# Winograd convolution with batch normalisation on one core: first weight loads in halves, no filling matmuls, last stores on three queues

## The chip, the cores and the metric

The kernel runs on one NeuronCore of a Trainium2 chip. A core has five engines with instruction streams of their own: TensorE (PE) multiplies matrices, VectorE (DVE) and ScalarE (ACT) work elementwise and can read the accumulators in PSUM, GpSimd (POOL) works elementwise on SBUF, and SyncE (SP) issues DMA transfers. ACT and POOL can issue transfers too. Each engine works through its own list in order and waits on semaphores for the others.

The metric is the device time of one execution in microseconds (us). Three executions of the kernel before took 197.62, 198.06 and 198.07 us; the median, 198.06 us, is the time to compare with. The profiled execution has a span of 196.3 us from its first to its last instruction.

## What is computed

A one-dimensional convolution with three taps over 1024 channels, a batch normalisation, and SiLU:

```python
# x: (2, 2048, 1024), w: (3, 1024, 1024), mean/var/g/b: (1024,), all bf16
xp = jnp.pad(x, ((0, 0), (1, 1), (0, 0)))
y = sum(jnp.einsum('bsc,cd->bsd', xp[:, k:k + S, :], w[k]) for k in range(3))
inv_std = 1.0 / jnp.sqrt(var + 1e-5)
y = (y - mean) * (g * inv_std) + b
return silu(y)                       # (2, 2048, 1024) bf16
```

## The kernel before

The kernel is a Winograd convolution: six output rows (`R = 6`) are made from eight transformed inputs (`NJ = 8`), so that eight products do the work of eighteen. It has three stages.

**Stage 1, the transform of x.** Each batch of x comes in 17 windows of up to 128 rows (256 KB each, the window named 16 only 66 KB). The order is windows 1 to 16, then 0. A window is one or two "jobs": a full window is two jobs of four matmuls against the transform matrix `rm`, each followed by one copy from PSUM to `T_sb` on ACT or DVE. That is 33 jobs for each batch and 66 in all. The first 48 run before the first product; the last 18 are strewn among the products of the first unit.

```python
W0_AT = (3, 4, 5)
W0_USE = 10
W1_AT = (5, 8, 11)                   # stands unused here
AMONG = 18                           # jobs left for the first unit
XBUFS = 12                           # window buffers
SPARE = 160
WARM = {0: 17, 4: 3, 6: 3, 8: 5, 10: 5}
PARAMS = 24
...
for i, wi in enumerate(order):
    load_x(0, wi)                    # one window, issued by SP
    if i in W0_AT:
        load_w(0, (0, 2, 1)[W0_AT.index(i)])   # 256 output channels of one tap: 512 KB
...
def warm(bank, n):                   # matmuls on zeros whose result nobody reads
    for _ in range(n):
        nc.tensor.matmul(
            ps[:, bank, 512 - SPARE:512], lhsT=nothing[:, 0:P], rhs=nothing, start=True, stop=True
        )

def ahead(jobs, job_n):
    for job in jobs:
        if job_n in WARM:
            warm(job_n % 4 * 2, WARM[job_n])
        t_job(job, job_n % 4 * 2)
        if job_n == PARAMS:
            params()                 # PE turns the 32 rows of var, g, mean, b; ACT copies them
        if job_n == PARAMS + 2:
            scales()                 # scale and beta of the normalisation, on POOL
        if job_n == W0_USE:
            prepare_first(0)         # Winograd weights of the first 128 channels, on POOL and ACT
        job_n += 1
```

The four rows `var`, `g`, `mean`, `b` (8 partitions of 256 bytes each) are loaded by four transfers on the POOL queue.

**Stage 2, the products.** There are 16 units, one for each block of 128 output channels (`dc`, eight of them) and batch (`bi`, two). A unit has 8 products of 8 matmuls with 342 columns, the Winograd output combinations on ACT and DVE, and a SiLU on ACT that writes its rows to `yts[bi]`. POOL makes the weights of the next channel blocks meanwhile. A finished unit is turned by a transposing DMA on SP (`turn`) and stored by SP (`store`), except the last two.

**Stage 3, the end.** The last unit is cut into parts `a` (229 columns) and `b` (113 columns). The rows of the last but one unit (`prev`) and of `a` and `b` are turned on PE (`flip`), copied from PSUM to SBUF, and stored (`ship`). A store is a list of transfers with runs of 256 bytes (128 channels):

```python
a, b = Unit(dc, bi, 4, 0, SPLIT), Unit(dc, bi, 0, SPLIT, NB)     # both write yts[bi]
sp, ac, po = nc.sync, nc.scalar, nc.gpsimd                       # ac and po are not used below
...
oa, ob, op = (olast.tile([P, R, NK, P], BF16, name=f"o{q}") for q in range(3))
...
before.store()                                       # unit 13: six transfers on SP
...
prev.flip(op, full, (0, R - 1), 1, act)
for k in range(NK):
    prev.ship(op, full[k], k * P, rows, (sp, sp, sp))     # unit 14: five transfers
...
a.flip(oa, ablocks, (0, R - 1), 5, dve)
a.ship(oa, ablocks[0], 0, rows, (sp, sp))            # one transfer, 192 KB
a.ship(oa, ablocks[1], P, rows, (sp, sp))            # two: 144 KB, then 7.5 KB
b.flip(ob, bblocks, rows, 1, dve)
b.ship(ob, bblocks[0], SPLIT, rows, (sp, sp))        # two: 168 KB, then 0.5 KB
```

Of the kernel before, what the change touches and what calls it, by code (L numbers as in the profile page):

```python
# [11 lines left out]
BF16 = mybir.dt.bfloat16  # L12
# [3 lines left out]
P = 128  # L16
R = 6
NJ = 8
W0_AT = (3, 4, 5)
W0_USE = 10  # L20
W1_AT = (5, 8, 11)
AMONG = 18
XBUFS = 12
SPLIT = 229
SPARE = 160
WARM = {0: 17, 4: 3, 6: 3, 8: 5, 10: 5}
PARAMS = 24
WT = 21

@with_exitstack  # L30
def kernel(
# [10 lines left out]
    nc = tc.nc  # L42
    B, S, C = x.shape
    D = w.shape[2]
    CT, DC = C // P, D // P
    NB = -(-S // R)
# [24 lines left out]
    T_sb = tpool.tile([P, CT, NJ, NT], BF16, name="T_sb")  # L71

    rows = consts.tile([4 * DC, P], BF16, name="rows")
    dummy = consts.tile([P, 2], FP32, name="dummy")
    nc.vector.memset(dummy, 0.0)
    nothing = consts.tile([P, SPARE], BF16, name="nothing")
    nc.vector.memset(nothing, 0.0)
    nc.scalar.activation(dummy[:, 1:2], dummy[:, 0:1], ACT.Silu)

    def transform_matrix():  # L80
# [43 lines left out]
    def load_x(bi, wi):  # L124
        if wi == 0:
            xw = xfirst
            cut = (P - 1) // 16 * 16
            nc.sync.dma_start(out=xw[1:1 + cut, :], in_=x[bi, 0:cut, :])
            nc.sync.dma_start(out=xw[1 + cut:P, :], in_=x[bi, cut:P - 1, :])
        else:  # L130
            xw = xpool.tile([P, C], BF16, name="xw")
            lo = R * WT * wi - 1
            hi = min(lo + P, S)
            nc.sync.dma_start(out=xw[0:hi - lo, :], in_=x[bi, lo:hi, :])  # L134
        clock["dma"] += 730.0
        xwin[bi, wi] = xw, clock["dma"]
# [6 lines left out]
    def load_w(pair, k, half=None):  # L143

        if (pair, "tile") not in raw:
            raw[pair, "tile"] = wpools[pair % 2].tile([P, 3, CT, 2, P], BF16, name=f"wch{pair % 2}")
        wch = raw[pair, "tile"]
        h0, h1 = (0, 2) if half is None else (half, half + 1)
        cols = slice((2 * pair + h0) * P, (2 * pair + h1) * P)
        nc.sync.dma_start(  # L150
            out=wch[:, k, :, h0:h1].rearrange("p c h d -> p c (h d)"), in_=w_all[:, k, :, cols]
        )
        clock["dma"] += 1200.0 * (h1 - h0)
        for h in range(2):
            raw[2 * pair + h] = wch[:, :, :, h]
# [74 lines left out]
    ident = consts.tile([P, P], BF16, name="ident")  # L230
    make_identity(nc, ident)

    for q, ap in enumerate((var, g, mean, b)):
        nc.gpsimd.dma_start(out=rows[q * DC:(q + 1) * DC, :], in_=ap.rearrange("(dc p) -> dc p", p=P))

    def params():

        v = ps[:, 7].bitcast(BF16)[:, 0:4 * DC]
# [15 lines left out]
    def t_jobs(bi):  # L254

        for wi in order:
            n = LAST if wi == NW - 1 else WT
            rows = min(P, S - (R * WT * wi - 1))
            n0 = bi * NB + wi * WT
            nb = 1 if CT * NJ * n <= 512 else 2  # L260
            nct = CT if nb == 1 else CT // 2
            for c0 in range(0, CT, nct):
                yield xwin[bi, wi], rows, n, n0, c0, nct, nb
# [30 lines left out]
    class Unit:  # L294
# [6 lines left out]

        def __init__(self, dc, bi, b0, lo=0, hi=NB):
            self.dc, self.bi, self.b0, self.lo, self.hi = dc, bi, b0, lo, hi
            self.bank = [ps[:, b0 + q, lo:hi] for q in range(4)]
            self.low, self.mid, self.high = (ps[:, b0 + q:b0 + q + 2, lo:hi] for q in range(3))
            self.yT = yts[bi]

        def product(self, q, j, add, between):  # L310
            dc = self.dc
# [164 lines left out]
    for i, wi in enumerate(order):  # L476
        load_x(0, wi)
        if i in W0_AT:
            load_w(0, (0, 2, 1)[W0_AT.index(i)])

    def warm(bank, n):

        for _ in range(n):
            nc.tensor.matmul(
                ps[:, bank, 512 - SPARE:512], lhsT=nothing[:, 0:P], rhs=nothing, start=True, stop=True
            )

    def ahead(jobs, job_n):
        for job in jobs:
            if job_n in WARM:  # L490
                warm(job_n % 4 * 2, WARM[job_n])
            t_job(job, job_n % 4 * 2)
            if job_n == PARAMS:
                params()
            if job_n == PARAMS + 2:
                scales()
            if job_n == W0_USE:
                prepare_first(0)
            job_n += 1
# [2 lines left out]
    ahead(jobs0, 0)  # L502
    for i, wi in enumerate(order):
        load_x(1, wi)
    jobs1 = list(t_jobs(1))
    ahead(jobs1[:-AMONG], len(jobs0))

# [29 lines left out]
            before.store()  # L537
        before, prev = prev, unit
    dc, bi = seq[-1]
    a, b = Unit(dc, bi, 4, 0, SPLIT), Unit(dc, bi, 0, SPLIT, NB)  # L540
    sp, ac, po = nc.sync, nc.scalar, nc.gpsimd
    rows = tuple(range(R))
    full = [(k * P, P, k) for k in range(NK)]
    ablocks, bblocks = [(0, P, 0), (SPLIT - P, P, 1)], [(SPLIT, NB - SPLIT, 0)]
    oa, ob, op = (olast.tile([P, R, NK, P], BF16, name=f"o{q}") for q in range(3))
    dve, act = nc.vector.tensor_copy, nc.scalar.copy
    a.scratch()
    b.scratch(a)
# [11 lines left out]
    b.plus(0, 3, between, 4.0)  # L560
    prev.flip(op, full, (0, R - 1), 1, act)
    for k in range(NK):
        prev.ship(op, full[k], k * P, rows, (sp, sp, sp))
    a.plus(2, 5, between)
    b.minus_one(between)
    a.minus_half(between)
# [9 lines left out]
    b.last(between)  # L576
    a.flip(oa, ablocks, (0, R - 1), 5, dve)
    a.ship(oa, ablocks[0], 0, rows, (sp, sp))
    a.ship(oa, ablocks[1], P, rows, (sp, sp))
    b.flip(ob, bblocks, rows, 1, dve)  # L580
    b.ship(ob, bblocks[0], SPLIT, rows, (sp, sp))

_INS = ['x', 'w', 'mean', 'var', 'g', 'b']
_OUTS = [((2, 2048, 1024), 'bfloat16')]
# [24 lines left out]
```

## Time and profile before

| what | value |
|---|---|
| median time of three executions | 198.06 us |
| span of the profiled execution | 196.3 us |
| PE busy | 181.5 us (92% of the span) |
| DVE, ACT, POOL busy | 155.2, 112.3, 138.3 us |
| read from HBM, written to HBM | 14.82 MB, 8.39 MB |
| copies of the transform jobs on ACT | 37 of 744 ns each |
| copies of the transform jobs on DVE | 29 of 844 ns each |
| matmuls of the transform jobs | 256, 25.5 us busy |

"Busy" is the time in which an engine works on an instruction. It says little alone: an engine that is idle costs time only where it is what the others wait for. The chain that ended last, followed back from the last instruction, says what the time was spent on in sequence. The time line gives the start and the length of each instruction or run of equal instructions; transfers appear there with the time that the issuing engine took to issue them ("SPq", or "POOL ... DMA_DIRECT2D"), not with the time of the data. The data are seen in the table of windows, whose last two columns are the mean share of the 16 DMA engines and the GB/s moved. In that table "PEclk" is the granted TensorE clock, 1.00 being full.

### The profile page before, as it was taken

How to read it: one execution, taken by the hardware profiler on the slowest of the kernel's cores; microseconds unless marked ns; L12 is line 12 of the kernel's file. 1: busy time of each engine (PE TensorE's matmuls, PEld its weight loads, DVE VectorE, ACT ScalarE, POOL GpSimd, SP SyncE). 2: the span in 40 equal slices, each digit the busy share in tenths (PEclk: the TensorE clock that was granted, in tenths of full speed). 3: DMA queues.
4: the chain of work that ended last, by engine and by line, in shares of the span. 5: the costliest groups of instructions: out<-in, count | busy, mean ns of one | idle time of the engine just before them, and what ended most of it. 6: DMA issues, size and time to landing. Idle time of an engine off the chain costs nothing.

```text
span 196.3 us, 3770 instructions
## 1 busy us (share of the span) xinstructions
PE 181.5 (92%) x1430; PEld 129.6 (66%) x1430; DVE 155.2 (79%) x222; ACT 112.3 (57%) x187; POOL 138.3 (70%) x80
## 2 busy tenths in 40 slices
PE   7549899999999999999999999999999999999860
PEld 6439677766666666666666666666666666679750
DVE  6636896589978799998798899889689978664760
ACT  3539897783628383547546554556273635468460
POOL 8149999962799669999999999999997750000000
PEclk9966999999999999999999999999999999999995
DMA  5999896029060929398849467959659291929644
GB/s 180 323 347 341 291 355 227 0 80 244 3 120 3 185 44 206 85 293 196 158 91 207 91 140 206 274 114 186 118 111 181 50 203 38 208 45 190 135 96 94
DMA packets 83702, 31.71 MB, mean 162 GB/s; under 512 B 67236, under 2 KB 79524, under 8 KB 83684
## 3 DMA queue, kind: packets, MB, share of 16 engines
q1 hardware_dynamic: 83556, 31.47, 67.4%
q8 instruction: 11, 0.18, 0.4%
q14 instruction: 7, 0.06, 0.1%
q0 software_dynamic: 128, 0.01, 0.0%
HBM read 14.82 MB, written 8.39 MB: 118 GB/s over the span
## 4 chain that ended last, share of the span: by engine, by line
PE 84%; SPq 4%; DMA 3%; ACT 3%; DVE 2%; issue 1%; ACTq 0%; DVEq 0%
PE ps L318 74%; PE ps L272 9%; DMA xw<-in_x_dram 3%; SPq L134 3%; ACT yT_145 L341 1%; PE ps L426 1%; DVE T_sb L285 1%; ACT T_sb L283 1%; SPq L150 1%; DVE ps L336 1%; ACT o_2156 L427 0%; DVE o_2155 L427 0%; ACTq L604 0%; ACT pc L329 0%; PE ps L239 0%
## 5 line engine op out<-in xcount | busy, mean ns | idle before, releaser
L329 ACT COPY pc<-ps 128x342 f32<-128x342 f32 (+2 forms) x34 | 14.5, 427 | 32.1 <-PE ps L318 29.5
L283 ACT CAST T_sb<-ps 128x672 bf16<-128x672 f32 (+1 forms) x37 | 26.1, 744 | 11.4 <-PE ps L272 11.2
L285 DVE CAST T_sb<-ps 128x672 bf16<-128x672 f32 (+1 forms) x29 | 23.5, 844 | 10.8 <-PE ps L272 10.3
L272 PE MATMUL ps<-rm,xw 128*128 128x168 bf16 (+1 forms) x256 | 25.5, 246 | 5.6 <-DMA xw<-in_x_dram 4.8
L272 PEld LDWEIGHTS <-xw 128*128 128x128 bf16 (+1 forms) x256 | 20.8, 103 | 10.7 <-DMA xw<-in_x_dram 6.3
L341 ACT ACTIVATE yT_145<-ps,beta,scale 128x342 bf16<-128x342 f32 (+5 forms) x27 | 18.4, 689 | 7.6 <-PE ps L318 7.6
L336 DVE SCALAR_TENSOR_TENSOR ps<-ps,pc 128x342 f32<-128x342 f32 (+2 forms) x34 | 16.9, 498 | 7.3 <-PE ps L318 5.7
L341 ACT ACTIVATE yT_144<-ps,beta,scale 128x342 bf16<-128x342 f32 (+1 forms) x24 | 17.4, 732 | 5.9 <-PE ps L318 5.9
L336 DVE SCALAR_TENSOR_TENSOR sd<-pc,ps 128x342 f32<-128x342 f32 (+2 forms) x17 | 8.3, 488 | 14.7 <-ACT sd L329 14.7
L329 ACT COPY sd<-ps 128x342 f32<-128x342 f32 (+2 forms) x17 | 7.3, 429 | 9.9 <-PE ps L318 9.8
L331 ACT ACTIVATE pc<-ps 128x342 f32<-128x342 f32 (+2 forms) x17 | 7.5, 441 | 9.4 <-PE ps L318 5.8
L318 PE MATMUL ps<-T_sb,wch_1539 128*128 128x342 bf16 (+2 forms) x80 | 10.8, 279 | 0.5 <-DVE ps L336 0.4
L318 PE MATMUL ps<-T_sb,wch_156 128*128 128x342 bf16 x64 | 10.6, 308 | 0.0
L318 PE MATMUL ps<-T_sb,wch_1121 128*128 128x342 bf16 x64 | 10.6, 307 | 0.0
L318 PE MATMUL ps<-T_sb,wch_710 128*128 128x342 bf16 x64 | 10.6, 307 | 0.0
L318 PEld LDWEIGHTS <-wch_1539 128*128 128x128 bf16 x80 | 7.1, 97 | 3.2 <-issue 0.9
L318 PEld LDWEIGHTS <-wch_156 128*128 128x128 bf16 x64 | 6.2, 97 | 3.1
L318 PEld LDWEIGHTS <-wch_710 128*128 128x128 bf16 x64 | 6.2, 97 | 3.1
L318 PEld LDWEIGHTS <-wch_1121 128*128 128x128 bf16 x64 | 6.2, 97 | 3.1
L198 POOL TENSOR_TENSOR u_700<-e_698,w1x_696 128x1024 bf16<-128x1024 f32 x2 | 4.2, 2132 | 5.7 <-DVE e_698 L180 5.7
L178 POOL TENSOR_TENSOR e_274<-wch_156 128x1024 f32<-128x1024 bf16 x1 | 2.1, 2113 | 6.5 <-DMA wch_156<-in_w_dram 6.5
L318 PE MATMUL ps<-T_sb,u_276 128*128 128x342 bf16 x32 | 6.1, 308 | 0.3 <-DVE T_sb L285 0.3
(262 smaller groups left out, 494.6 us busy)
## 6 DMA issues: line engine op xcount, KB each, us to landing
xw<-in_x_dram SPq DMA_DIRECT2D x30, 256.0 KB
out_dram<-o SPq DMA_DIRECT2D x28, 192.0 KB
out_dram<-o SPq DMA_DIRECT2D x14, 120.0 KB
wch_156<-in_w_dram SPq DMA_DIRECT2D x3, 512.0 KB
wch_710<-in_w_dram SPq DMA_DIRECT2D x3, 512.0 KB
wch_1121<-in_w_dram SPq DMA_DIRECT2D x3, 512.0 KB
wch_1539<-in_w_dram SPq DMA_DIRECT2D x3, 512.0 KB
xfirst<-in_x_dram SPq DMA_DIRECT2D x2, 224.0 KB
```

Of the source, the lines that this page charges most:

```text
L134: nc.sync.dma_start(out=xw[0:hi - lo, :], in_=x[bi, lo:hi, :])
L150: nc.sync.dma_start(out=wch[:, k, :, h0:h1].rearrange("p c h d -> p c (h d)"), in_=w_all[:, k, :, cols])
L178: eng.tensor_tensor(e, w0, w2, op=ALU.add)
L198: nc.gpsimd.tensor_tensor(u[:, i], sums[dc, q], o, op=op)
L272: nc.tensor.matmul(v[:, c * nb // nct, c % (nct // nb)], lhsT=xw[0:rows, (c0 + c) * P:(c0 + c + 1) * P], rhs=rm[0:rows, :, 0:n], start=Tru ...
L283: nc.scalar.copy(dst, src)
L285: nc.vector.tensor_copy(dst, src)
L318: nc.tensor.matmul(self.bank[q], lhsT=lhsT, rhs=T_sb[:, ct, j, nsl], start=not add and ct == 0, stop=ct == CT - 1, skip_group_check=add,)
L329: nc.scalar.copy(dst, self.bank[q])
L331: nc.scalar.mul(dst, self.bank[q], by)
L336: nc.vector.scalar_tensor_tensor(out=out, in0=in0, scalar=scalar, in1=in1, op0=ALU.mult, op1=op1)
L341: nc.scalar.activation(self.yT[:, rows, self.lo:self.hi], src, ACT.Silu, bias=beta[:, dc:dc + 1], scale=scale[:, dc:dc + 1])
```

## The change

The change rearranges the start and the end of the kernel; the middle stays as it is.

- At the start, the weights of the first 256 channels are loaded in halves of 128 channels: three transfers of 256 KB for the channels used first (after windows 4, 6 and 8 of the count from 0, in place of three of 512 KB after 3, 4 and 5), and the other three among the windows of the second batch. This lets more windows of x come before the weights.
- The matmuls on zeros are left out.
- The four parameter rows are issued first thing on the ACT queue and turned right after the first job (in place of after job 24), and their arithmetic on POOL comes after job 4.
- The first weights are prepared after job 18 in place of job 10.
- At the end, the five stores of the last but one unit are issued by POOL, one of the last unit's small stores by POOL and one by ACT. This is to have several issuers in place of one.
- The last unit writes its rows to a buffer of its own, and the three output tiles lie in the weight tile that is free by then.

```diff
-W0_AT = (3, 4, 5)
-W0_USE = 10
+W0_AT = (4, 6, 8)
+W0_USE = 18
 W1_AT = (5, 8, 11)
-SPARE = 160
-WARM = {0: 17, 4: 3, 6: 3, 8: 5, 10: 5}
-PARAMS = 24
 [...]
     rows = consts.tile([4 * DC, P], BF16, name="rows")
+    for q, ap in enumerate((var, g, mean, b)):
+        nc.scalar.dma_start(out=rows[q * DC:(q + 1) * DC, :], in_=ap.rearrange("(dc p) -> dc p", p=P))
     dummy = consts.tile([P, 2], FP32, name="dummy")
     nc.vector.memset(dummy, 0.0)
-    nothing = consts.tile([P, SPARE], BF16, name="nothing")
-    nc.vector.memset(nothing, 0.0)
 [...]
-    for q, ap in enumerate((var, g, mean, b)):
-        nc.gpsimd.dma_start(out=rows[q * DC:(q + 1) * DC, :], in_=ap.rearrange("(dc p) -> dc p", p=P))
 [...]
-        def __init__(self, dc, bi, b0, lo=0, hi=NB):
+        def __init__(self, dc, bi, b0, lo=0, hi=NB, yT=None):
-            self.yT = yts[bi]
+            self.yT = yts[bi] if yT is None else yT
 [...]
         if i in W0_AT:
-            load_w(0, (0, 2, 1)[W0_AT.index(i)])
+            load_w(0, (0, 2, 1)[W0_AT.index(i)], 0)
-    def warm(bank, n):
-        [...]
     def ahead(jobs, job_n):
         for job in jobs:
-            if job_n in WARM:
-                warm(job_n % 4 * 2, WARM[job_n])
             t_job(job, job_n % 4 * 2)
-            if job_n == PARAMS:
+            if job_n == 0:
                 params()
-            if job_n == PARAMS + 2:
+            if job_n == 4:
                 scales()
 [...]
         load_x(1, wi)
+        if i in W1_AT:
+            load_w(0, W1_AT.index(i), 1)
 [...]
-    a, b = Unit(dc, bi, 4, 0, SPLIT), Unit(dc, bi, 0, SPLIT, NB)
+    yT = olast.tile([P, R, NBP], BF16, name="yTlast")
+    a, b = Unit(dc, bi, 4, 0, SPLIT, yT), Unit(dc, bi, 0, SPLIT, NB, yT)
 [...]
-    oa, ob, op = (olast.tile([P, R, NK, P], BF16, name=f"o{q}") for q in range(3))
+    free = (DC // 2) % 2
+    turned = wpools[free].tile([P, 3, CT, 2, P], BF16, name=f"wch{free}").rearrange("p k c h d -> p (k c h) d")
+    op, oa, ob = (
+        turned[:, R * lo:R * hi].rearrange("p (i k) d -> p i k d", i=R)
+        for lo, hi in ((0, NK), (NK, NK + 2), (NK + 2, NK + 3))
+    )
 [...]
-        prev.ship(op, full[k], k * P, rows, (sp, sp, sp))
+        prev.ship(op, full[k], k * P, rows, (po, po, po))
 [...]
-    a.ship(oa, ablocks[1], P, rows, (sp, sp))
+    a.ship(oa, ablocks[1], P, rows, (sp, po))
 [...]
-    b.ship(ob, bblocks[0], SPLIT, rows, (sp, sp))
+    b.ship(ob, bblocks[0], SPLIT, rows, (sp, ac))
```

More of the change, by code (lines that the diff above doesn't have):

```diff
@@ L478 @@
         if i in W0_AT:
-            load_w(0, (0, 2, 1)[W0_AT.index(i)])
-    def warm(bank, n):
[L483 to L486, printed above, removed]
+            load_w(0, (0, 2, 1)[W0_AT.index(i)], 0)
     def ahead(jobs, job_n):
         for job in jobs:
-            if job_n in WARM:
-                warm(job_n % 4 * 2, WARM[job_n])
             t_job(job, job_n % 4 * 2)
-            if job_n == PARAMS:
+            if job_n == 0:
                 params()
-            if job_n == PARAMS + 2:
+            if job_n == 4:
                 scales()
```

## The prediction

> **What bounds the kernel now.** I read the page first, for the busy shares and for the chain that ended last. The second line is the chain by line: L318 is the products, L272 the transform of x.
>
> ```profile
> PE 181.5 (92%) x1430; PEld 129.6 (66%) x1430; DVE 155.2 (79%) x222; ACT 112.3 (57%) x187; POOL 138.3 (70%) x80
> PE ps L318 74%; PE ps L272 9%; DMA xw<-in_x_dram 3%; SPq L134 3%; ACT yT_145 L341 1%; PE ps L426 1%; DVE T_sb L285 1%; ACT T_sb L283 1%; SPq L150 1%; DVE ps L336 1%; ACT o_2156 L427 0%; DVE o_2155 L427 0%; ACTq L604 0%; ACT pc L329 0%; PE p
> ```
>
> The products are three quarters of the span. Then I read the same chain in order of time (start us, length us, what), to see where it leaves PE.
>
> ```profile
> 8.15 6.79 DMA xw<-in_x_dram
> 14.99 4.24 PE ps L272 x36
> ...
> 30.25 0.30 PE ps L318
> ...
> 43.66 134.97 PE ps L318 x936
> ```
>
> From 43.66 to 178.63 PE does nothing but 936 matmuls of products, 144 ns each. The change touches no instruction there, so that block moves as a whole. What can change is the start, up to the first product at 30.25, and the end, after 178.63.
>
> At the start a window of x is waited for until 14.99. The time line of PE (start, length, what, idle before) shows how the windows come: windows 5, 6 and 7 at 10.07, 12.54 and 14.99. One transform takes 0.76 us at the first and 1.30 us at the others.
>
> ```profile
> 7.57 0.51 PE L484 MATMUL ps<-nothing 128*128 128x160 bf16 x5
> 10.07 0.76 PE L272 MATMUL ps<-rm,xw 128*128 128x168 bf16 x8 [1.99 <-DMA xw<-in_x_dram]
> 12.54 1.30 PE L272 MATMUL ps<-rm,xw 128*128 128x168 bf16 x8 [1.37 <-DMA xw<-in_x_dram]
> 14.99 1.30 PE L272 MATMUL ps<-rm,xw 128*128 128x168 bf16 x8 [1.15 <-DMA xw<-in_x_dram]
> ```
>
> After 14.99 no wait for x is left: the copies bound it (ACT 744 ns, DVE 844 ns, side by side 1/(1/744 + 1/844) = 396 ns a job). Six windows, 12 jobs, are done by then. The other 36 take 36 x 0.396 = 14.2 us, and ACT's two preparing instructions (1.06 and 1.04 us, shared by two engines) 1.05 us: 14.99 + 15.3 = 30.3. The first product starts at 30.25, so the account closes.
>
> How fast data move I took from the table of windows; the last two columns are the DMA share and GB/s. At 43 to 48 only weights with runs of 512 bytes are moved, at 14 to 17 mostly x with runs of 2 KB, at 182.5 to 184 stores with runs of 256 bytes.
>
> ```profile
> 43.00:48.00 5.00, 4.99 (x35) 3.21 (x34) 4.25 (x7) 2.89 (x5) 0.00 (x0) 1.00 1.16 306
> 14.00:17.00 3.00, 2.01 (x15) 2.01 (x16) 1.41 (x2) 2.79 (x5) 2.64 (x3) 0.50 1.06 389
> 182.50:184.00 1.50, 1.49 (x23) 1.47 (x22) 0.74 (x3) 0.21 (x1) 0.00 (x0) 1.00 1.00 214
> ```
>
> The DMA engines are full in all three, and shorter runs carry less. At the end the time line of SP shows the issuing (start, length).
>
> ```profile
> 187.62 0.63 SPq L448 DMA_DIRECT2D out_dram<-o_2156  x1
> 189.82 2.52 SPq L442 DMA_DIRECT2D out_dram<-o_2154  x3
> 192.45 0.62 SPq L442 DMA_DIRECT2D out_dram<-o_2155  x1
> 193.12 0.65 SPq L448 DMA_DIRECT2D out_dram<-o_2155  x1
> ```
>
> SP had finished the last but one unit's stores at 188.25 and waited for `oa`. The copy of `ob` ends at 191.20 (190.64 + 0.56), but its store is issued at 192.45, behind three others.
>
> **What the Trainium skill says.**
>
> - "DMA: Bandwidth & Descriptors", section "Why small descriptors are slow (HBM only)": each packet costs a fixed extra, some 27% at 256 bytes. The trace agrees in direction: 214 GB/s at 256 bytes, 306 at 512, 389 at 2 KB. This bears on the halves: 256 KB then come in 256-byte runs.
> - The same page, section "Issuing engines are not separate DMA queues": several issuers save only the time of issuing. Here that time is about 0.65 us each, and only those after 191.20 count.
> - The same page, section "SWDGE vs HWDGE vs iDMA": descriptors of POOL's transfers are computed by its own cores in software. The four small ones of this kernel take 0.52 to 0.76 us each on POOL, for 8 partitions of 256 bytes; no line shows one with 768 pieces, as a store of 128 rows by 6 has.
> - "TensorE: Matmul & The Clock Gate", section "Part 1: The HAM clock gate (the "warmup" mystery)": half the clock until about 3.4 us of sustained work. The trace agrees: 0.76 against 1.30 us for the same eight matmuls, at a granted clock of 1.00 and 0.50.
>
> **The change part by part.**
>
> *Weights in halves.* By the rates above a window takes 0.262 MB / 389 = 0.67 us of transfer, a 512 KB load 0.524 / 306 = 1.71 us, and a half, if loads of 256-byte runs go like stores (an estimate), 0.262 / 214 = 1.22 us. Window 7 came after 7 windows and 3 loads, 9.86 us of transfer, at 14.99; so 5.1 us are start and delay. The check: window 5 at 5 x 0.674 + 1.71 + 5.1 = 10.2 (seen 10.07), window 6 at 12.6 (seen 12.54). With the change, window 5 comes at 8.5, 6 at 10.4, 7 at 11.0, 8 at 12.9, 9 at 13.6, and 10, behind three halves, at 10 x 0.674 + 3.67 + 5.1 = 15.5. Window 25, the last that the 48 jobs need, comes behind four halves at about 26.3, in time. So at 15.5 not 12 but 18 jobs are done. 30 jobs are left: 30 x 0.396 + 1.05 = 12.9, and the first product starts at 28.4 in place of 30.25: **-1.8 us at best**.
>
> *Parameters first.* PE, in order, stands after job 0 until four transfers issued by ACT have landed. Issuing takes about 0.45 us each, as SP's first do, from 0.72 to 2.5. The same rows took 5.6 to 6.9 us from issue to landing on POOL's queue, but amid full traffic; at the very start I take 3 us. PE then waits until about 5.5 with window 1 half done. ACT's table load (1.28 us) moves behind the issues and still ends before the first copy at 4.55. This is hidden as long as PE catches up by 15.5.
>
> *No matmuls on zeros.* 33 matmuls go, all in waits; that gives nothing back. What they bought was the clock: without them the first windows run at 1.30 us. From 5.5, five windows are ready or near, and PE works at the slow clock for one or two of its windows, until 9 to 12, then faster than the data come. Costs 0 to 1.1 us (the 0.55 us that each of two windows loses), if PE is slow again when window 10 comes.
>
> *Preparation.* POOL needs taps 0 and 2: 7 windows and 2 halves, 4.7 + 2.4 + 5.1 = 12.3, against 11.93 before. Its last weights are done at 32.6 before; they are first used at 39.13, or 37.3 with the change. No wait. The arithmetic of the scales (32.58 to 35.83 before) moves into idle time of POOL.
>
> The start in sum: between -1.8 and 0, middle **-1.2**.
>
> *The end.* On SP, two stores are left ahead of `ob`, the second of them at 190.80 for 0.65 us, and `ob`'s own can follow at about 191.5 in place of 192.45; the last row goes by ACT at the same time. -0.95 us, if POOL is not late. POOL has been idle since 159.7. It gets five stores from 182.07 on, with 2048 pieces (768 + 768 + 480 + 30 + 2), and `oa`'s 7.5 KB after those. At 1 us each it ends near 187 and nothing is seen of it. At 2 us each it ends at 192, its small one is issued at 192.6, and the end stays where it was; slower still and it becomes the end. I take 0.6 for no harm and 0.4 for an end later by 0.5: 0.6 x -0.95 + 0.4 x 0.5 = **-0.4**.
>
> *Own buffer, reused weight tile.* The last unit writes rows first at 185.62, while the turning of unit 13 out of the shared buffer was issued at 174.54 and its stores by 184.55. Nobody waited. The reused tile's last readers are three units back. Zero.
>
> Sum: -1.2 - 0.4 = -1.6, from 198.06 to 196.5.
>
> **The rivals.**
>
> 1. *The halves cost as much as whole loads.* If 256-byte loads run at 150 GB/s, a half takes 1.75 us, window 10 comes at 17.1, and the start gains 0.2 us. For it: the 214 GB/s are of stores, and no line shows a load with such short runs; and the other three halves must be loaded too. Then about 197.6.
> 2. *The parameters hold PE up.* If the rows land at 8 or 9 as POOL's did, PE starts at the slow clock with its backlog and warms near 13. About 9 jobs are then done, and 39 x 0.396 + 1.05 end at 29.5 to 30.6. Together with a neutral end: 198 to 199.
> 3. *POOL's descriptors become the end.* At 4 us a full store, three of them last beyond 193, and what follows lands after 195. Then the end is 1 to 3 us later: 198 to 200. Against it: the end has 7 us for POOL's five stores.
> 4. *Everything fits and PE stays fast*: -1.8 - 0.95, 195.3.
>
> **Range and chances.** One more sign: the kernel before still carries `W1_AT`, `ac` and `po`, names that only the other arrangement uses. So that arrangement was probably there first, and was left for something quicker. This lifts my middle by 0.3 us, to 196.8. Low 194.6 is rival 4 with a little more; high 200.4 holds rivals 2 and 3 together. 2% is 4 us: faster than 194.1 would need more than all gains, slower than 202.0 two failures with their full size. Chances 0.07, 0.87, 0.06.
>
> **What would show it.** Right: window 10 starts on PE near 15.5 with 18 jobs done; the first product between 28 and 29.5; the block of products as long as before; `ob`'s store issued within 0.4 us of its copy. Wrong: PE standing behind the parameter transpose after 7; windows of 1.30 us beyond 13; waits for x after 16; POOL issuing past 190, or a last landing that belongs to POOL. If the block of products is longer than 135 us, a wait for POOL's weights has come in that I have not seen.

## The result and the profile after

| | kernel before | changed kernel |
|---|---|---|
| median time | 197.97 us (4 executions beside the changed one) | 195.06 us (4 executions) |
| ratio, with 95% interval | 1 | 0.985 (0.982 to 0.988) |
| span of the profiled execution | 196.3 us | 193.4 us |
| first product | 30.25 us | 27.82 us |
| first product to start of the last copy (`ob`) | 160.39 us | 160.46 us |
| start of that copy to the end of the span | 5.66 us | 5.12 us |

The changed kernel is 2.9 us quicker, where 1.3 us were forecast (198.06 to 196.8). The table cuts the span into three stretches: the start gives 2.43 us, the middle nothing, the end 0.54 us.

The page of the changed kernel has the same bound as before, with a larger share of the products and of the waiting for x, since everything else at the start has shrunk (busy shares, then the chain that ended last, by line; L312 is the products, L266 the transform).

```profile
PE 178.5 (92%) x1397; PEld 126.5 (65%) x1397; DVE 157.2 (81%) x221; ACT 111.8 (58%) x187; POOL 141.2 (73%) x82
PE ps L312 75%; DMA xw<-in_x_dram 8%; PE ps L266 5%; SPq L131 2%; ACT yTlast L335 2%; ACT T_sb L277 1%; PE ps L420 1%; SPq L147 1%; DVE ps L330 1%; ACT w1x_295 L163 0%; DVE T_sb L279 0%; ACT wch_2123 L421 0%; DVE wch_2123 L421 0%; ACT pc L323 0%; ACT w1x_298 L181 0%
```

The chain in order of time (start, length, what) shows a second wait for x, which the kernel before did not have on its chain: it ends at 26.50.

```profile
8.71 5.65 DMA xw<-in_x_dram
14.40 0.48 PE ps L266 x4
...
20.39 6.11 DMA xw<-in_x_dram
...
40.11 136.17 PE ps L312 x944
```

The block of products starts 3.55 us earlier and is 1.20 us longer, for it now holds 944 matmuls and not 936 (so its 136.17 us are no sign of a new wait); both blocks run at 144 ns a matmul, and they end 2.35 us apart. So it moved as a whole.

The time line of PE at the start (start, length, what, idle before and its releaser):

```profile
3.92 0.72 PE L266 MATMUL ps<-rm,xw 128*128 128x168 bf16 x4 [3.92 <-DVE rm L101]
5.13 0.18 PE L233 MATMUL ps<-ident,rows 32*128 32x32 bf16 x1 [0.49 <-DMA rows<-in_b_dram]
5.24 5.92 PE L266 MATMUL ps<-rm,xw 128*128 128x168 bf16 x48
...
14.40 2.15 PE L266 MATMUL ps<-rm,xw 128*128 128x168 bf16 x24 [1.04 <-DMA xw<-in_x_dram]
...
26.54 1.14 PE L266 MATMUL ps<-rm,xw 128*128 128x168 bf16 x12 [0.90 <-DMA xw<-in_x_dram]
27.82 0.31 PE L312 MATMUL ps<-T_sb,u_292 128*128 128x342 bf16 x1
```

Four readings. The parameters cost PE 0.49 us at 5.13, and it has no pause in the next 5.92 us, so that is caught up. Window 10 arrives at 14.40, not at 15.5, with 18 jobs done. No pause for the parameters is left in the stretch that the copies bound. And PE waits 0.90 us for a window at 26.54, just ahead of the first product.

The time line at the end, by issuing engine (length is the time of issuing, not of the data):

```profile
180.03 3.12 POOL L436 DMA_DIRECT2D out_dram<-wch_2123  x4 [21.70 <-ACT wch_2123 L421]
182.90 0.80 POOL L442 DMA_DIRECT2D out_dram<-wch_2123  x1
...
187.47 2.00 SPq L436 DMA_DIRECT2D out_dram<-wch_2123  x3
187.73 0.60 POOL L436 DMA_DIRECT2D out_dram<-wch_2123  x1 [4.04 <-DVE wch_2123 L421]
188.28 0.56 DVE L421 COPY wch_2123<-ps 113x768 bf16<-113x768 bf16 x1 [0.84 <-PE ps L420]
188.87 0.71 ACTq L442 DMA_DIRECT2D out_dram<-wch_2123  x1
```

POOL issues four stores, of 768, 768, 480 and 30 pieces, in 3.12 us and one of 2 pieces in 0.80, so the number of pieces hardly shows in the time of issuing; it is through at 183.70. SP's third store, that of `ob`, follows the copy (which ends at 188.84) without a pause, where it used to be issued 1.25 us behind it.

### The profile page after: what moved, and what is told of

It is laid out like the page before. It is cut to its first block, busy times and chain, and to the rows that moved or that the text cites. A ratio compares the mean times of both kernels' runs of the same rounds, so it can differ in the third digit from the quotient of the medians.

```text
span 193.4 us, 3708 instructions
## 1 busy us (share of the span) xinstructions
PE 178.5 (92%) x1397; PEld 126.5 (65%) x1397; DVE 157.2 (81%) x221; ACT 111.8 (58%) x187; POOL 141.2 (73%) x82
## 4 chain that ended last, share of the span: by engine, by line
PE 81%; DMA 8%; ACT 4%; SPq 2%; DVE 1%; issue 1%; DVEq 0%
PE ps L312 75%; DMA xw<-in_x_dram 8%; PE ps L266 5%; SPq L131 2%; ACT yTlast L335 2%; ACT T_sb L277 1%; PE ps L420 1%; SPq L147 1%; DVE ps L330 1%; ACT w1x_295 L163 0%; DVE T_sb L279 0%; ACT wch_2123 L421 0%; DVE wch_2123 L421 0%; ACT pc L323 0%; ACT w1x_298 L181 0%
## 5 line engine op out<-in xcount | busy, mean ns | idle before, releaser
L266 PE MATMUL ps<-rm,xw 128*128 128x168 bf16 (+1 forms) x256 | 26.0, 249 | 7.7 <-DVE rm L101 3.9
L279 DVE CAST T_sb<-ps 128x672 bf16<-128x672 f32 x29 | 23.6, 854 | 8.3 <-PE ps L266 8.3
L266 PEld LDWEIGHTS <-xw 128*128 128x128 bf16 (+1 forms) x256 | 21.0, 104 | 12.7 <-DMA xw<-in_x_dram 6.9
L436 POOL DMA_DIRECT2D out_dram<-wch_2123 x5 | 3.7, 833 | 25.7 <-ACT wch_2123 L421 21.7
L335 ACT ACTIVATE yT_142<-ps,beta,scale 128x342 bf16<-128x342 f32 (+1 forms) x24 | 17.4, 731 | 5.9 <-PE ps L312 5.9
L335 ACT ACTIVATE yT_143<-ps,beta,scale 128x342 bf16<-128x342 f32 (+1 forms) x21 | 15.4, 732 | 5.9 <-PE ps L312 5.9
L330 DVE SCALAR_TENSOR_TENSOR sd<-pc,ps 128x342 f32<-128x342 f32 (+2 forms) x17 | 8.3, 487 | 12.8 <-ACT sd L323 12.7
L312 PE MATMUL ps<-T_sb,wch_1507 128*128 128x342 bf16 (+2 forms) x80 | 10.8, 280 | 0.5 <-DVE ps L330 0.4
L312 PE MATMUL ps<-T_sb,wch_678 128*128 128x342 bf16 x64 | 10.6, 308 | 0.0
L312 PE MATMUL ps<-T_sb,wch_1089 128*128 128x342 bf16 x64 | 10.6, 308 | 0.0
L312 PE MATMUL ps<-T_sb,wch_156 128*128 128x342 bf16 x64 | 10.6, 308 | 0.0
L312 PEld LDWEIGHTS <-wch_1507 128*128 128x128 bf16 x80 | 7.1, 97 | 3.2 <-issue 0.9
L312 PEld LDWEIGHTS <-wch_678 128*128 128x128 bf16 x64 | 6.2, 97 | 3.1
L312 PEld LDWEIGHTS <-wch_156 128*128 128x128 bf16 x64 | 6.2, 97 | 3.1
L312 PEld LDWEIGHTS <-wch_1089 128*128 128x128 bf16 x64 | 6.2, 97 | 3.1
L312 PE MATMUL ps<-T_sb,u_292 128*128 128x342 bf16 x32 | 6.1, 308 | 0.1
```

Of the source, the lines that this page charges most:

```text
L266: nc.tensor.matmul(v[:, c * nb // nct, c % (nct // nb)], lhsT=xw[0:rows, (c0 + c) * P:(c0 + c + 1) * P], rhs=rm[0:rows, :, 0:n], start=Tru ...
L279: nc.vector.tensor_copy(dst, src)
L312: nc.tensor.matmul(self.bank[q], lhsT=lhsT, rhs=T_sb[:, ct, j, nsl], start=not add and ct == 0, stop=ct == CT - 1, skip_group_check=add,)
L330: nc.vector.scalar_tensor_tensor(out=out, in0=in0, scalar=scalar, in1=in1, op0=ALU.mult, op1=op1)
L335: nc.scalar.activation(self.yT[:, rows, self.lo:self.hi], src, ACT.Silu, bias=beta[:, dc:dc + 1], scale=scale[:, dc:dc + 1])
L436: queues.pop(0).dma_start(out=outs[c0 * R:c1 * R].rearrange("(p i) d -> p i d", i=R)[:, every], in_=o[c0 - t:c1 - t, every, k],)
```

## The experiments

A difference in us below is one minus the ratio, times the kernel before of the same chip; brackets hold its 95% interval. The theories A and B are named in each expectation. The first product of one profiled execution varies by up to 0.9 us (in three kernels whose start is that of before: 30.25, 29.74, 30.62), so it takes several profiles, or the time, to tell small differences.

### Which half of the change brings the time

*Halves alone*: the kernel before with the loads of the changed one, but with its zero matmuls and its place for the parameters.

```diff
-W0_AT = (3, 4, 5)
-W0_USE = 10
+W0_AT = (4, 6, 8)
+W0_USE = 18
-            load_w(0, (0, 2, 1)[W0_AT.index(i)])
+            load_w(0, (0, 2, 1)[W0_AT.index(i)], 0)
         load_x(1, wi)
+        if i in W1_AT:
+            load_w(0, W1_AT.index(i), 1)
```

> The kernel before, with the halved first loads alone (and the preparation after job 18). Theory A (the halves are cheap, about 0.8 us each, and make nearly the whole gain of the start): window 10 starts on PE near 14.4, the first product near 27.8 in place of 30.25, time about 2.3 us lower. Theory B (the early parameters and the missing zero matmuls share in it, a half costs the 1.22 us of my prediction): window 10 near 15.5, first product near 29, time about 1.2 us lower.

195.86 us, ratio 0.989 (0.986 to 0.992): 2.2 us quicker [1.5 to 2.8]. The time line of PE shows window 10 at 14.17 and the first product at 27.78.

```profile
14.17 0.75 PE L272 MATMUL ps<-rm,xw 128*128 128x168 bf16 x8 [1.00 <-DMA xw<-in_x_dram]
...
27.78 0.30 PE L318 MATMUL ps<-T_sb,u 128*128 128x342 bf16 x1
```

The eight matmuls of a window take 0.75 us here, against 1.30 us at the same place in the kernel before. The halves are the largest part, and window 10 is early in this kernel too.

*The end alone*: the kernel before with the last stores on three queues.

```diff
-        prev.ship(op, full[k], k * P, rows, (sp, sp, sp))
+        prev.ship(op, full[k], k * P, rows, (po, po, po))
-    a.ship(oa, ablocks[1], P, rows, (sp, sp))
+    a.ship(oa, ablocks[1], P, rows, (sp, po))
-    b.ship(ob, bblocks[0], SPLIT, rows, (sp, sp))
+    b.ship(ob, bblocks[0], SPLIT, rows, (sp, ac))
```

> The kernel before, with the three issuers at the end alone (output tiles and buffers as before). Theory A (the transfers take the place of the wait for the issuer): the last store is issued 1.2 us sooner after its copy, but the span from that copy's start to the end shrinks from 5.66 to about 5.1 us only, time 0.5 us lower. Theory B (only issuing counts, as I predicted for its good case): 0.95 us lower or more. Theory C (POOL's transfers disturb): 0 or higher. First product unchanged at 30.2 under all.

196.91 us, ratio 0.995 (0.992 to 0.997): 1.0 us quicker [0.5 to 1.5]. From the start of `ob`'s copy to the end are 4.90 us, 0.76 less than in the kernel before.

*The start alone*: the changed kernel with all last stores on SP (the reverse of the diff above).

> The changed kernel with all its last stores issued by SP again, so that only its start is changed. Theory A (the three issuers fill the pause between the last unit's stores, worth 0.4 to 1.0 us): from the last copy's start to the end 5.2 to 5.7 us in place of 4.8 to 5.1; time 0.4 to 1.0 us above the changed kernel, 2.0 to 2.5 us below the kernel before. Theory B (the end gives nothing once the start is early): as the changed kernel within 0.2 us.

194.68 us, ratio 0.982 (0.980 to 0.984): 3.6 us quicker than before [3.2 to 4.0], and no slower than the changed kernel. Its last stretch is longer, 5.33 us, and the table of windows (from:to, length, busy of PE, PEld, DVE, ACT, POOL, PEclk, DMA share, GB/s) shows why: a pause of the transfers while the last store waits to be issued.

```profile
187.75:189.50 1.75, 0.00 (x0) 0.00 (x0) 0.28 (x1) 0.00 (x0) 0.00 (x0) 0.86 0.86 188
189.50:190.25 0.75, 0.00 (x0) 0.00 (x0) 0.00 (x0) 0.00 (x0) 0.00 (x0) 0.50 0.19 42
190.25:191.25 1.00, 0.00 (x0) 0.00 (x0) 0.00 (x0) 0.00 (x0) 0.00 (x0) 0.50 0.79 164
```

So the trace has the gain of the end, and the time of this pair doesn't resolve it. Over all profiles with the full output, that stretch takes 4.84 to 5.13 us with three issuers (seven profiles, mean 4.97) and 5.21 to 5.68 us with one (nine profiles, mean 5.48). The ranges don't overlap; I take the difference, 0.51 us, for the end's worth.

*All but the halves*: the changed kernel with its first loads whole.

```diff
-W0_AT = (4, 6, 8)
-W0_USE = 18
+W0_AT = (3, 4, 5)
+W0_USE = 10
-            load_w(0, (0, 2, 1)[W0_AT.index(i)], 0)
+            load_w(0, (0, 2, 1)[W0_AT.index(i)])
-        if i in W1_AT:
-            load_w(0, W1_AT.index(i), 1)
```

> The changed kernel with the first weights loaded whole again (after windows 4, 5 and 6, preparation after job 10); early parameters, no zero matmuls and the three issuers stay. Theory A (the halves make the whole gain of the start): the first product goes back to 30.2 to 30.8 and only the gain of the end is left, 0.5 to 1.0 us below the kernel before. Theory B (the early parameters and the scales on an idle POOL bring something of their own): first product near 29.3, 1.5 us or more below.

196.92 us, ratio 0.994 (0.992 to 0.996): 1.2 us quicker than before [0.8 to 1.7], with the first product at 29.29. Since about 0.5 us of that is the end, the early parameters and the missing zero matmuls bring something together, where I had put a cost.

### What a half costs

*Later weights in halves*: in the kernel before, each of the later loads of 512 KB becomes two of 256 KB. In that stretch nothing but weights moves, so it measures loads with 256-byte runs by themselves.

```diff
-                load_w(i // 4 + 1, k)
+                load_w(i // 4 + 1, k, 0)
+                load_w(i // 4 + 1, k, 1)
```

> The kernel before, with the later weight loads (three of 512 KB at about 43 us, when nothing else moves) made as six of 256 KB with runs of 256 bytes. This measures the disputed cost by itself. Theory A: the loads run at about 300 GB/s, as the 512-byte ones (306), a half in about 0.85 us, all done in about 5 us. Theory B: at the 214 GB/s of the stores, a half in 1.22 us, all done in over 7 us. The time of the whole kernel should not move, as PE has other work there.

One execution, 198.0 us, the time of before (198.12). The same window as was shown of the kernel before (there 306 GB/s):

```profile
43.00:48.00 5.00, 5.00 (x36) 3.25 (x34) 4.26 (x6) 3.06 (x6) 0.00 (x0) 1.00 0.98 210
```

Alone, loads with such runs move at 210 GB/s, close to the 214 of the stores that I had borrowed; six took 7.7 us, 1.28 us each. The estimate holds where only halves move (with the engines less full, a DMA share of 0.98 beside 1.16). But there are windows of x among them at the start.

*Pairs of halves at the start*: in the kernel before, each early load of 512 KB becomes two halves at the same place. The bytes and the order stay, only the runs get shorter.

```diff
-            load_w(0, (0, 2, 1)[W0_AT.index(i)])
+            load_w(0, (0, 2, 1)[W0_AT.index(i)], 0)
+            load_w(0, (0, 2, 1)[W0_AT.index(i)], 1)
```

> The kernel before with each of the first three loads made as two halves issued one after the other, at the same places: the same bytes in the same order, only in runs of 256 in place of 512 bytes. Measured alone, halves ran at 210 GB/s, but in the changed kernel windows came as if a half cost 0.8 us. Theory A (in a full stream the short runs cost next to nothing, bytes alone count): windows 5, 6 and 7 at 10.1, 12.5 and 15.0 as before, within 0.4 us, and the same time. Theory B (a half costs 1.22 us wherever it stands): windows at 10.8, 14.0 and 17.2, first product near 32, time 1.5 to 2 us higher.

199.14 us, ratio 1.005 (1.003 to 1.008): 1.1 us slower [0.7 to 1.5]. Window 7, behind six halves, arrives at 15.57; in eight profiles with whole loads it arrives at 14.57 to 15.12, mean 14.79.

```profile
12.60 0.75 PE L272 MATMUL ps<-rm,xw 128*128 128x168 bf16 x8 [1.83 <-DMA xw<-in_x_dram]
15.57 6.64 PE L272 MATMUL ps<-rm,xw 128*128 128x168 bf16 x52 [2.21 <-DMA xw<-in_x_dram]
```

So by the arrival six halves cost 0.8 us more than three whole loads, 0.13 us each, and not 2.2 us as the rates alone would have it (this is one profile against eight). What that makes of a half depends on what is held fixed. With the prediction's fixed time for "start and delay" held, a half is worth 0.855 + 0.13 = 0.98 us (0.855 is half of a whole load's 1.71), and the prediction's own sum, with the 4.9 us of delay that 14.79 stands for, gives window 10 at 10 x 0.674 + 3 x 0.98 + 4.9 = 14.6. Seven profiles with the halves and the whole output have it at 14.17 to 15.24, mean 14.65.

The distance between two waits needs no fixed time, and it gives a dearer half. Above, one window and two halves lie between 12.60 and 15.57: (2.97 - 0.674) / 2 = 1.15 us. In the kernel with the start alone, two windows and a half lie between these two waits:

```profile
12.03 1.51 PE L266 MATMUL ps<-rm,xw 128*128 128x168 bf16 x16 [1.00 <-DMA xw<-in_x_dram]
14.59 2.15 PE L266 MATMUL ps<-rm,xw 128*128 128x168 bf16 x24 [1.05 <-DMA xw<-in_x_dram]
```

That is 2.56 - 2 x 0.674 = 1.21 us, nearly the 1.22 of the prediction; five profiles have these two waits 2.51 to 2.56 us apart. Read so, the half was priced about right, and the fixed time is shorter with halves in the stream: 14.65 - 10 x 0.674 - 3 x 1.21 = 4.3 us in place of 5.1. Whichever term is blamed, the sum put window 10 0.85 us too late; why the stream with halves is ahead of it I have not shown.

### The zero matmuls

The kernel before with `WARM = {}`.

> The kernel before, without the matmuls on zeros. My prediction charged up to 1.1 us for their absence. Theory A: they fill waits for x only, and PE is at the slow clock from 11.2 to 17.9 with them as well, so the first product stays within 0.3 us of 30.25 and the time within 0.4 us. Theory B: the slow clock costs 0.5 us or more; first product at 30.8 or later.

198.36 us over 22 executions, ratio 1.001 (1.000 to 1.003): 0.3 us slower [0.0 to 0.5]. The Trainium skill, "TensorE: Matmul & The Clock Gate", section "Part 1: The HAM clock gate (the "warmup" mystery)", ties the full clock to sustained work; the fillers did not hold it here. With them the granted clock stood at 0.77 from 10 to 12 us, at 0.50 up to 16 and at 0.52 up to 18; without them at 0.61 from 12 to 14, at 0.50 up to 18 and at 0.68 up to 20. Either way this adds up to about 6.8 us at half the clock. The fillers moved the slow stretch and did not end it. What they are worth in this kernel is a quarter of a us.

The changed kernel has no such stretch. This is the line of the granted clock on four pages (40 slices of the span, in tenths): the kernel before, halves alone, all but the halves, and the changed kernel.

```profile
PEclk9966999999999999999999999999999999999995
PEclk9996999999999999999999999999999999999995
PEclk9996999999999999999999999999999999999996
PEclk9999999999999999999999999999999999999997
```

All seven profiles with the changed start are like the last line, and all ten others have a dip in the third to fifth slice. (The two nines at the start of the last line are not borne out by the matmuls: 48 from 5.24 take 5.92 us, 123 ns each, where 24 from 14.40 take 2.15 us, 90 ns each.) So PE was at full clock when window 10 came, without any matmul on zeros. Neither the halves alone nor the rest of the change without them gives this; which parts it takes, and what it is worth in time, no run here separates.

### The parameters

*Early parameters alone*: the kernel before with the four rows issued by ACT at the start, turned after job 0 and computed after job 4.

```diff
+    for q, ap in enumerate((var, g, mean, b)):
+        nc.scalar.dma_start(out=rows[q * DC:(q + 1) * DC, :], in_=ap.rearrange("(dc p) -> dc p", p=P))
-    for q, ap in enumerate((var, g, mean, b)):
-        nc.gpsimd.dma_start(out=rows[q * DC:(q + 1) * DC, :], in_=ap.rearrange("(dc p) -> dc p", p=P))
-            if job_n == PARAMS:
+            if job_n == 0:
-            if job_n == PARAMS + 2:
+            if job_n == 4:
```

> The kernel before with the parameters alone moved to the front (rows issued first thing by ACT, turned after job 0, scales after job 4); whole loads, zero matmuls and one issuer stay. In the kernel before the parameter transpose after job 24 stands in the copy-bound stretch: PE waits 0.70 us for it, and DVE and ACT sit idle 0.63 and 0.56 us around it. Theory A (that gap is on the path, and the early place is free): the two gaps go, first product about 0.6 us sooner than the 29.7 to 30.7 of the other kernels with this start, time 0.4 to 0.7 us lower. Theory B (my prediction: the move gives nothing, and its wait for the rows costs): 0 or higher.

197.03 us, ratio 0.994 (0.991 to 0.996): 1.2 us quicker [0.7 to 1.7]. I had given this part zero. What I had overlooked stands in the time line of the kernel before, in the stretch where the copies set the pace:

```profile
21.46 0.17 PE L239 MATMUL ps<-ident,rows 32*128 32x32 bf16 x1 [0.70 <-ACT T_sb L283]
...
21.67 0.19 ACT L240 COPY prm<-ps 128x32 bf16<-128x32 bf16 x1 [0.35 <-PE ps L239]
22.06 8.46 ACT L283 CAST T_sb<-ps 128x672 bf16<-128x672 f32 x12 [0.21 <-PE ps L272]
22.35 8.60 DVE L285 CAST T_sb<-ps 128x672 bf16<-128x672 f32 x11 [0.63 <-PE ps L272]
```

PE's transpose needs a place in PSUM and waits for ACT's copy; the transform matmuls queue behind it; DVE then stands 0.63 us and ACT 0.56 us (0.35 + 0.21). Work of 0.17 and 0.19 us stops both engines that bound the stretch, for 0.6 us.

*The parameters in a wait for x*: one figure of the kernel before, `PARAMS = 11` in place of 24, so that the transpose lies among the waits for windows. The arithmetic on POOL is then listed after job 13, but still runs behind the weights (from 32.16 us, where it was 32.58).

> The kernel before with the parameter transpose after job 11 in place of job 24, the rows still loaded by POOL: it then falls into the wait for window 7 and not into the copy-bound stretch. Moving the parameters to the very front lowered the time by 1.2 us (0.7 to 1.7), and the trace of the kernel before shows a gap of 0.6 us only. Theory A (the gap in the copy-bound stretch is the whole cost of the late place): 0.6 to 1.2 us below the kernel before here too, no idle time of DVE and ACT around 21 us. Theory B (the early load by ACT, or POOL's early scales, share in it): 0.3 us or less. If the rows land after 11, PE waits for them, but in a wait for x anyway.

197.72 us over 22 executions, ratio 0.997 (0.996 to 0.998): 0.6 us quicker [0.3 to 0.8], as long as the gap. The two engines copy without a pause from 20.5 on:

```profile
19.63 10.59 ACT L283 CAST T_sb<-ps 128x672 bf16<-128x672 f32 x15 [0.35 <-PE ps L272]
...
20.52 10.13 DVE L285 CAST T_sb<-ps 128x672 bf16<-128x672 f32 x13 [0.59 <-PE ps L272]
```

The times show 0.6 us of the gain as the gap; this one profile doesn't, as its first product comes at 29.94, within the spread of the start of before. The 0.35 and 0.59 us in brackets are waits for PE at the slow clock, which was 0.51 from 18 to 20 us. The other 0.6 us of the early parameters (with about as much uncertainty) stay open.

*The parameters twice*: meant as a double dose of that gap.

```diff
-            if job_n == PARAMS:
+            if job_n in (PARAMS, PARAMS + 8):
```

> The kernel before with the parameter transpose and its copy done a second time, after job 32. The dose test for the gap: theory A, each costs what the first does, 0.6 us by the trace, so 0.4 to 0.8 us above the kernel before (up to 1.2 if the early-parameter run measured the gap alone). Theory B (the gap is made up for later, before the first product): within 0.2 us.

209.69 us, ratio 1.058 (1.055 to 1.060): 11.4 us slower, and a failure as a dose. The second copy overwrites `prm`, which POOL's arithmetic still has to read, and POOL does that only after the weights:

```profile
35.32 0.18 ACT L240 COPY prm<-ps 128x32 bf16<-128x32 bf16 x1 [10.41 <-POOL beta L251]
35.56 5.69 PE L272 MATMUL ps<-rm,xw 128*128 128x168 bf16 x50 [9.60 <-ACT prm L240]
```

The experiment made a wait for a reader, 10 us long, and says nothing on the gap.

### The new wait at 26.54

The changed kernel with its second halves later among the windows of the second batch: `W1_AT = (9, 11, 13)` in place of `(5, 8, 11)`.

> The changed kernel with the second halves after windows 9, 11 and 13 of the second batch in place of 5, 8 and 11. In the changed kernel PE waits 0.9 us for a window at 26.5, behind a second half issued at 22.45 or before. Theory A (that wait is on the path, and the halves in front of the window make it): it goes away, the first product starts 0.4 to 0.8 us sooner, time 0.4 to 0.8 us below the changed kernel, 3.3 to 3.8 us below the kernel before. Theory B (the window is late because its buffer came free late, or the copies are as far behind anyway): first product unchanged within 0.2 us. Theory C (POOL's second preparation then starts too late): a wait in the first units, time higher.

194.73 us, ratio 0.983 (0.980 to 0.986). The wait is gone, and the first product comes at 26.72:

```profile
21.11 5.56 PE L266 MATMUL ps<-rm,xw 128*128 128x168 bf16 x60
...
26.72 0.30 PE L312 MATMUL ps<-T_sb,u 128*128 128x342 bf16 x1
```

So the second halves cause it. The time is not apart from that of the changed kernel, so its cost is at most about half a us.

### What bounds the end

*POOL's stores back on SP*: the changed kernel with `prev.ship(..., (sp, sp, sp))`; the two small stores stay on POOL and ACT.

> The changed kernel with the five stores of the last but one unit issued by SP again; the last tiles keep their three issuers. Theory A (SP has time for them, as it sat idle before the last unit's first store in the kernel before): same time within 0.3 us, POOL's share in the gain is nil. Theory B (POOL takes a load off SP that mattered): 0.5 us or more higher than the changed kernel.

194.52 us, ratio 0.982 (0.979 to 0.985), last stretch 4.84 us: POOL neither harms nor helps. So what the end gains lies with the two small stores.

*One store less*: the changed kernel without the first store of `a`. It leaves out 192 KB of the output, to see whether the last store waits for the transfers ahead of it.

```diff
-    a.ship(oa, ablocks[0], 0, rows, (sp, sp))
```

> The changed kernel without the first store of the last unit (192 KB of the output are left out). In the changed kernel the DMA engines are full from 188.7 to 191.5. Theory A (the end is now bound by the transfers): from the last copy's start to the end about 0.7 to 0.9 us less than the 4.8 to 5.1 of the kernels with three issuers, as 192 KB take 0.9 us at 210 GB/s. Theory B (the end is the last store's own issue, delay and landing): the same stretch, within 0.2 us.

193.86 us, ratio 0.978 (0.975 to 0.981); the last stretch takes 4.40 us, 0.57 less than the mean of 4.97. The windows at its end:

```profile
188.25:189.25 1.00, 0.00 (x0) 0.00 (x0) 0.11 (x1) 0.00 (x0) 0.00 (x0) 1.00 0.74 156
189.25:189.75 0.50, 0.00 (x0) 0.00 (x0) 0.00 (x0) 0.00 (x0) 0.00 (x0) 0.53 0.15 35
189.75:190.75 1.00, 0.00 (x0) 0.00 (x0) 0.00 (x0) 0.00 (x0) 0.00 (x0) 0.50 0.75 155
```

Set them beside the changed kernel, where no such pause is left:

```profile
188.50:190.00 1.50, 0.00 (x0) 0.00 (x0) 0.34 (x1) 0.00 (x0) 0.00 (x0) 1.00 0.76 161
190.00:191.50 1.50, 0.00 (x0) 0.00 (x0) 0.00 (x0) 0.00 (x0) 0.00 (x0) 0.75 0.88 181
191.50:193.00 1.50, 0.00 (x0) 0.00 (x0) 0.00 (x0) 0.00 (x0) 0.00 (x0) 0.50 0.05 13
```

In the changed kernel the stores of `oa` are still moving when that of `ob` is issued, and these 504 KB (192, 144 and 168) share the DMA engines. Taking 192 KB away frees 0.57 us and uncovers the last store's own delay again. The Trainium skill, "DMA: Bandwidth & Descriptors", section "Issuing engines are not separate DMA queues", says that more issuers save only the time on the sequencer; this agrees: 0.95 us of issuing were to be saved, and 0.51 us remained.

### Both together, and the changed kernel again

*Later second halves and stores on SP*: `W1_AT = (9, 11, 13)` and `prev.ship(..., (sp, sp, sp))`, the candidate for a better version.

> The changed kernel with the second halves after windows 9, 11 and 13 and the five stores of the last but one unit back on SP: the two variants that each came out at or below the changed kernel. Theory A (the window waited for at 26 is on the path): first product near 26.7, time 0.3 to 0.8 us below the changed kernel. Theory B (no gain beyond noise): within 0.3 us of it.

194.61 us, ratio 0.980 (0.978 to 0.982), first product 27.33.

*The changed kernel, unaltered*, on another chip beside the kernel before:

> The changed kernel itself, in more rounds than the four executions of its first measurement, as the variants with some of the change undone came out at or a little below it. Theory A (its true gain is about 1.8%, start 1.8% less nothing for the end): ratio 0.980 to 0.984, time as with all stores on SP. Theory B (POOL's transfers cost the changed kernel something): 0.9847 again, 0.3 us or more above the variant with the stores back on SP.

194.55 us, ratio 0.982 (0.979 to 0.984): 3.6 us quicker [3.1 to 4.1], beside the 3.0 us [2.5 to 3.6] of the first comparison; first product 27.34. The candidate is not apart from it: no version that beats the changed kernel was shown.

### The parts side by side

| part of the start | us by time | from |
|---|---|---|
| weights in halves | -2.2 [-2.8 to -1.5] | halves alone |
| early parameters | -1.2 [-1.7 to -0.7] | alone |
| no zero matmuls | +0.3 [0.0 to 0.5] | alone |
| sum | -3.1 | |
| all three | -3.6 [-4.0 to -3.2] | the start alone |

The sum and the whole agree within their uncertainty, so that a gain of the parts together, such as the missing slow stretch, is neither shown nor excluded by the times. By the trace, the first product comes at 30.2 us with the start of before (mean of those three profiles) and at 27.3 us with that of the changed kernel (mean of five), 2.9 us earlier. With 0.51 us of the end this makes 3.4 us.

## Why the prediction was off

The place and the direction were right, and the size was not: a start of -1.2 us was forecast and -2.9 us came. Point by point:

- **The bound, and the block of products that moves as a whole:** right. The stretch from the first product to the copy of `ob` is 160.39 and 160.46 us.
- **Halves let more windows come first:** right, with 18 jobs done when window 10 is waited for. The sum "10 x 0.674 + 3.67 + 5.1 = 15.5" was mis-sized: window 10 came at 14.65 (mean), 0.85 us earlier. By the distance between waits the half was about right (1.15 to 1.21 us for the 1.22 that had been borrowed from stores) and what failed is the fixed 5.1 us, which had been fitted to a stream of whole loads and is 4.3 us here; by the arrival alone it could as well be the half (0.98 us). Rival 1, a half as dear as a whole, is out.
- **No zero matmuls, "costs 0 to 1.1 us":** the range held, the discount taken from it did not. It lowered the best case from -1.8 to -1.2, for the case that PE is slow again when window 10 comes. PE was not: the granted clock was full there in all seven profiles with the changed start. By itself, in the kernel before, leaving the fillers out cost 0.3 us; in the whole change nothing of it is seen. This is another 0.6 us.
- **Parameters first, "hidden":** half right. The wait at the new place is hidden, as I had put it (0.49 us at 5.13, where rival 2 had PE waiting until 8 or 9). But I asked only what the new place costs, and not what the old one did: there were 0.6 us of idle copies around 21. My account of the kernel before closed within 0.1 us without that gap because its pace was too slow. The 744 and 844 ns are the lengths of single copies, whose records overlap; in the lines above the copies follow each other every 705 and 782 ns (8.46 / 12 and 8.60 / 11), which side by side is 371 ns a job and not 396. 36 jobs at 371 ns with the 1.05 us of preparing are 14.4 us and not 15.3; the gap and other waits of the copies filled the rest. A sum that closed hid a term.
- **"Window 25 ... at about 26.3, in time":** wrong. PE waited until 26.54, 0.90 us in that profile, and 0 to 0.44 us in the four others with this start. So the last windows come without slack, and part of the gain is given back.
- **Start in sum:** 1.2 + 0.6 (discount) + 0.85 (window 10) = 2.65. From window 10 to the first product 12.9 us were forecast and 12.7 came (mean of five): the faster pace, 30 x 0.371 + 1.05 = 12.2, less what the wait near 26 takes. The two kernels without that wait take 11.9 and 12.1 us. Together this is the 2.9 us seen, within 0.1.
- **Preparation of the weights, own buffer, reused tile:** right, no wait. POOL's last first weights are done at 32.04 and PE does not wait for them.
- **The end, -0.4:** right in size (-0.51) and wrong in its make-up. I had mixed -0.95 without harm from POOL and +0.5 with it. POOL took about 0.8 us a store, so rival 3 falls; but the full -0.95 did not come either, because `ob`'s transfer, issued at once, then shares the DMA engines with those ahead of it.
- **0.3 us added for unused names in the kernel before:** wrong. Here they said nothing about the time.

Rival 4, "everything fits and PE stays fast", had the mechanism: 195.3. The 195.06 us beside it agree partly by chance, since its window 10 came too late and its end was too good.

Open: the other 0.6 us of the early parameters; which of the two terms made window 10 early; what takes the slow stretch away and what that is worth; the 0.9 us by which the first product varies between profiles of the same start (the slow stretch lies elsewhere in each); and the time, not the trace, of the end, which was 1.0 us in the end alone and nothing between the start alone and the changed kernel.

## What to carry to other kernels

When an operation is moved, price the place it leaves as well as the place it goes to: look for the idle time of the engines that bound that stretch, right behind it in the time line. A sum that reproduces the time before does not prove that no term is missing, for its rates were fitted to the same trace: take a pace from the starts of successive instructions, not from the mean length of one. A fixed delay that was fitted to one order of transfers need not hold for another; the distance between two waits gives the price of a transfer without it.

## What had not been expected of the hardware

- Loads with 256-byte runs moved at 210 GB/s alone (1.28 us for 256 KB), and by the distance between waits took 1.15 to 1.21 us each between windows with 2 KB runs.
- POOL issued stores of 30 to 768 pieces in about 0.8 us each (four in 3.12 us) and one of 2 pieces in 0.80 us.
- Two instructions of 0.17 and 0.19 us stopped two copying engines for 0.6 us.
- Zero matmuls in the waits were worth 0.3 us; in the kernel before, about 6.8 us at half the clock lay between 10 and 20 with them and without them. The changed kernel, which has none, was at full clock from 10 us to the last stretch.
